# Smaller TensorE tiles in the two transform steps of an H3 long convolution, with kv kept by channels in two buffers

## The chip, the cores and the metric

The kernel runs on one core of a Trainium2 chip. The metric is the device time of one execution in microseconds; 718.91 us is the median of three executions before the change (717.91 to 720.57). Everything is computed in 32-bit floats. Where a profile is quoted, PE is TensorE's matmuls, PEld its weight loads, DVE VectorE, ACT ScalarE, POOL GpSimd, and SP the engine whose queue issues most of the DMAs.

## The reference

The input `q` has S = 2048 tokens and D = 640 channels. The kernel computes an H3 block (a causal long convolution per channel, gated) and then a mixer MLP over the token axis, both modulated by vectors worked out from `c`. The part that the change touches is the first:

```
h  = layernorm(q) * (1 + ca) + sa
kv = (short causal convolution of k with shift_k, 4 taps) * v
y  = causal convolution over all 2048 tokens of kv with ssm_k, channel by channel,  + kv * ssm_D
x  = q + ga * h * y
out = x + gb * MLP_over_tokens(layernorm(x) * (1 + cb) + sb)
```

The reference does the long convolution with a real FFT of length 4096. The MLP has 1728 hidden units with a tanh-GELU.

## The kernel before

**The order of the work.** The order of all instructions is written by hand: each engine runs its own queue in the order in which the Python code issues it, and the SP queue issues DMAs in that order too. The 640 channels are taken in NC = 5 chunks of 128. The loop of line 511 does one chunk per iteration c: it transforms chunk c and brings it back, and in between does part of the work of chunk c + 1 (step one of its transform) and of chunk c + 2 (its kv). After that loop come the layernorm, the two products of the MLP with their split weights (from line 656 on, which the change does not touch) and the output.

**The transform.** 2048 tokens are written as 64 x 32 (n1 = 64 rows on the partitions, n2 = 32), and the length-4096 transform becomes two matmul steps with constants.

- `step1(side, t)`, line 210: for kv (side 0, the tile X) and for ssm_k (side 1, a permuted copy KSP in the tile P), 32 column groups i, eight for each t. Each group has 2 x 64 rows on the partitions (two halves of the channels) and 64 columns, and is the stationary operand, [128 rows, 64 columns]; the moving operand is a 128-column half of F1, one call for the real and one for the imaginary part. So there are 4 x 8 x 2 = 64 calls per side and chunk. In X the 64 columns of a group lie 32 elements apart; KSP has them side by side. ACT evicts each t (1024 columns) into the tile Z (line 220).
- `f2(g)`, line 224, is step two: for each of eight frequencies k1, for real and imaginary part and for two channel halves h, one call with a stationary [128 rows, 64 columns] block of the constant W2 and 64 moving columns out of Z. W2 is block-diagonal over two halves c of the columns, so half of each block is zeros. One f2(g) has 32 calls; eight g make a chunk. ACT copies the ssm_k half of the result to `kt` (line 238); DVE multiplies it with the kv half in two operations of 512 columns into `p` (mul, line 242); `add` (line 248) subtracts and adds real and imaginary parts into `y`, two operations of 256 columns on POOL, except for the last g of a chunk after the first, which DVE does.
- `i2(r)`, line 255, and `i1(half)`, line 273, are the inverse steps. i2 uses tiles of 32 rows by 128 columns, i1 of 64 rows by 64 columns, with 64 moving columns in both. Row tiles at the same columns write to different PSUM banks there (the offsets 512 * (qd % 2) and 512 * e).

A call of `pe.matmul` on 32-bit floats becomes two weight loads and two matmuls in the trace: f2 makes 1280 calls in the five chunks, and the profile counts 2560 matmuls on line 234.

**kv and the other work.** `kv_ops(g)` (line 172) is eight operations of 512 columns on DVE for one of four token groups g; the last writes into X. All four groups of a chunk are 32 operations, handed out between other work by `dv(n)` (line 506); `kv_loads` (line 185) issues the k and v loads of the next chunk as the groups finish. For the first chunks POOL does group 2, with its own copy of the taps (PW). There is one X: the kv of the next chunk may only be written when step one of this one has read it. `load_ks` (line 150) loads ssm_k of a chunk into KSR (half of the tile T_aux) in pieces of 32 floats; `perm_add` adds ssm_D to the first tap (on POOL, in iteration c after g = 3), and `perm` (line 163) copies KSR to KSP on ACT. The next `load_ks` follows in each iteration (line 626) as soon as `perm` has read KSR. `gate` (line 299) multiplies the convolution with h on DVE and adds it to x on POOL. `load_rows` fetches MLP weights into T_aux near the end of the loop.

**The start.** Lines 443 to 502 load and compute kv of chunks 0 and 1, load W2 (two tiles of 2 MB), q and four fifths of the first half of `w_mod` (`mod_load`, two pieces of it into the tile that later takes the constant V1). V1 (2 MB, used by i1) is loaded in iteration 0 at line 561, after those pieces have been used.

Of the kernel before, what the change touches and what calls it, by code (L numbers as in the profile page):

```python
# [20 lines left out]
def _constants():  # L21
# [9 lines left out]
    w2 = np.zeros((2, 32, 2, 64, 2, 2, 32))  # L31
    for c in range(2):
        w2[0, :, c, :, 0, c] = np.cos(ang)
        w2[1, :, c, :, 0, c] = -np.sin(ang)
        w2[0, :, c, :, 1, c] = np.sin(ang)
        w2[1, :, c, :, 1, c] = np.cos(ang)
# [8 lines left out]
    return {"small": small.astype(np.float32), "w2": w2.reshape(128, 8192).astype(np.float32),  # L45
# [4 lines left out]
def mixer_kernel(ctx: ExitStack, tc: tile.TileContext, q, k, v, shift_k, ssm_k, ssm_D, w1, b1, w2, b2, c,  # L50
# [38 lines left out]
    KSP = P.rearrange("p (i m) -> p i m", i=32)  # L89
# [8 lines left out]
    W2 = [t.rearrange("p (k m) -> p k m", m=64) for t in T_w2]  # L98
# [64 lines left out]
    def perm(c):  # L163
        act.activation(KSP.rearrange("p i (n e) -> p i e n", e=2),
                       KSR.rearrange("p (e i n) -> p i e n", e=2, i=32), AF.Copy)

# [5 lines left out]
    def kv_ops(g, eng=dve):  # L172
# [8 lines left out]
        ops.append(lambda: TT(eng, X.rearrange("p (n i) -> p n i", i=64)[:, 8 * g:8 * g + 8], S_,  # L181
# [13 lines left out]
    def kv(c_next, gs=((0,), (1,), (2,), (3,))):  # L195

        ops = []
        for gl in gs:
            o = kv_ops(gl[0])

            def end(gl=gl, last=o.pop()):
                last()
                if c_next is not None:
                    for g in gl:
                        kv_loads(c_next, g)
            ops += o + [end]
        return ops


    def step1(side, t, later=False):  # L210

        ps = psum()
        for a in range(8):
            i = 8 * t + a
            lhs = KSP[:, i] if side else X.rearrange("p (m i) -> p i m", i=32)[:, i]
            o = 512 * (a % 2) + 128 * (a // 2)
            for ri in range(2):
                pe.matmul(ps[64 * ri:64 * ri + 64, o:o + 128], lhs, F1[:, 128 * ri:128 * ri + 128], start=True,  # L218
                          stop=True)
# [4 lines left out]
    def f2(g):  # L224

        ps = psum()
        for kk in range(8):
            k1 = 8 * g + kk
            for ri in range(2):
                for h in range(2):  # L230
                    o = 128 * kk + 64 * ri
                    rhs = bass.AP(tensor=T_z.tensor, offset=T_z.offset + 128 * h + 2 * k1,
                                  ap=[T_z.ap[0], [256, 32], [1, 2]])
                    pe.matmul(ps[64 * h:64 * h + 64, o:o + 64], W2[k1 // 32][:, 2 * (k1 % 32) + ri], rhs, start=True, stop=True)  # L234
# [13 lines left out]
        def add(eng=pool):  # L248
            for ri, t, op in ((0, pa, ALU.subtract), (1, pb, ALU.add)):
# [216 lines left out]
    run(kv_ops(2, pool))  # L466
    run(kv_ops(0))
    kv_loads(1, 0)
    run(kv_ops(1))
    kv_loads(1, 1)  # L470
    kv_loads(1, 2)
    run(kv_ops(3))
    sync.dma_start(T_w2[0], c_w2[:, 0:4096], max_dma_last_dim=4096)
    kv_loads(1, 3)
    sync.dma_start(T_w2[1], c_w2[:, 4096:8192], max_dma_last_dim=4096)
# [6 lines left out]
    perm(0)  # L482
    all_taps()
    load_taps(2)
    for t in range(4):
        step1(0, t)
    run(kv_ops(2, pool))
    run(kv_ops(0))
    run(kv_ops(1))
    for t in range(4):  # L490
        step1(1, t)
# [7 lines left out]
    pl = [three(t) for t in (T_aux, T_aux[:, 2048:3968], T_v1, T_v1[:, 1920:3840], P)]  # L499

    for kk in range(4):
        mod_load(0, kk, (T_aux[:, 0:1920], T_aux[:, 2048:3968], T_v1[:, 0:1920], T_v1[:, 1920:3840])[kk])

    fill = kv_ops(3)
# [6 lines left out]
    for c in range(NC):  # L511
# [26 lines left out]
        pa_next(dve if c else pool)  # L538
# [5 lines left out]
        if c and c + 2 < NC:  # L544
            taps()
            if c + 3 < NC:
                load_taps(c + 3)
        if c == 0:
            mod_load(0, 4, P[:, 0:1920])
            for t in range(4):  # L550
                step1(0, t)
# [9 lines left out]
            sync.dma_start(T_v1[:, 0:4096], c_v1, max_dma_last_dim=4096)  # L561
# [16 lines left out]
            run(kv_ops(2, pool))  # L578
# [5 lines left out]
            perm(1)  # L584
            load_ks(2)
            run(ac[8:16])
            run(po[0:2])
            fill.extend(kv(3, ((0,), (1, 2), (3,))))
        elif cn is not None:
            for t in range(2):  # L590
                step1(0, t)
            perm(cn)
# [492 lines left out]
```

## Time and profile before

| | us |
|---|---|
| median of three executions | 718.91 (717.91 to 720.57) |
| the profiled execution | 722.7 |
| its span, first to last instruction | 720.8 |
| loop over the chunks, from f2 of chunk 0 (42.0) to the end of f2 of chunk 4 (288.4) | 246.4 |
| of it f2, five times (25.0, 19.5, 19.0, 18.9, 19.1) | 101.5 |

The profile is of one execution. A row of a group says line, engine, operation, output<-inputs, shape, count | busy time, mean ns of one | idle time of the engine before it, and what ended that. For matmuls the shape starts with rows*columns of the stationary tile. In the timeline a row is: start, length, engine, line, operation, count, and in brackets the engine's idle time before it and what ended it; "issue" there means that the engine waited for nothing that the profile shows. In the table of stretches (windows) a row has: the stretch and its length; then busy time and count of each engine, the granted TensorE clock (1.00 is full speed), the busy share of the DMA engines and the GB/s moved.

### The profile page before, as it was taken

How to read it: one execution, taken by the hardware profiler on the slowest of the kernel's cores; microseconds unless marked ns; L12 is line 12 of the kernel's file. 1: busy time of each engine (PE TensorE's matmuls, PEld its weight loads, DVE VectorE, ACT ScalarE, POOL GpSimd, SP SyncE). 2: the span in 40 equal slices, each digit the busy share in tenths (PEclk: the TensorE clock that was granted, in tenths of full speed). 3: DMA queues.
4: the chain of work that ended last, by engine and by line, in shares of the span. 5: the costliest groups of instructions: out<-in, count | busy, mean ns of one | idle time of the engine just before them, and what ended most of it. 6: DMA issues, size and time to landing. Idle time of an engine off the chain costs nothing.

```text
span 720.8 us, 20751 instructions
## 1 busy us (share of the span) xinstructions
PE 656.0 (91%) x9131; PEld 632.6 (88%) x9131; DVE 492.6 (68%) x861; ACT 297.4 (41%) x465; POOL 154.6 (21%) x135
## 2 busy tenths in 40 slices
PE   0797968999999999998889999999999989999997
PEld 0797758989999989777889999999999989999997
DVE  7666748969879638788894313212389768888887
ACT  0432564645745545446766223112244222333221
POOL 5187038715626328100010000000000000000000
PEclk9998889999999899879999999999999999999999
DMA  9979998527233522351203543352263423455510
GB/s 185 243 223 223 304 235 172 116 52 164 57 68 87 168 55 70 112 133 44 53 7 59 101 75 60 76 100 59 59 183 102 141 96 123 130 159 175 159 45 37
DMA packets 165903, 84.89 MB, mean 118 GB/s; under 512 B 88979, under 2 KB 157366, under 8 KB 165814
## 3 DMA queue, kind: packets, MB, share of 16 engines
q1 hardware_dynamic: 161266, 82.27, 46.1%
q10 hardware_dynamic: 4548, 1.31, 1.0%
q8 instruction: 71, 1.16, 0.7%
q14 instruction: 18, 0.15, 0.1%
HBM read 73.07 MB, written 10.49 MB: 116 GB/s over the span
## 4 chain that ended last, share of the span: by engine, by line
PE 54%; DVE 23%; ACT 6%; issue 5%; POOL 5%; DMA 4%; SPq 2%; ACTq 0%; DVEq 0%; POOLq 0%
PE pst L432 21%; PE pst L218 8%; PE pst L234 8%; PE pst L1026 7%; PE pst L263 5%; DVE m_w L59 4%; POOL y L59 4%; DVE m_x L59 3%; PE pst L282 3%; DVE tap L59 2%; ACT m_w L939 2%; PE pst L951 2%; DVE kt L59 2%; DVE m_x L960 1%; DVE m_v L59 1%
## 5 line engine op out<-in xcount | busy, mean ns | idle before, releaser
L234 PE MATMUL pst<-z,w 128*64 128x64 f32 x2560 | 96.8, 241 | 11.2 <-ACT z L220 6.1
L234 PEld LDWEIGHTS pst<-z,w 128*64 128x64 f32 x2560 | 95.4, 142 | 12.9 <-ACT z L220 7.3
L59 POOL TENSOR_TENSOR y<-p 128x256 f32<-128x256 f32 x72 | 90.6, 1315 | 27.2 <-DVE p L59 26.7
L59 DVE TENSOR_TENSOR p<-pst,kt 128x512 f32<-128x512 f32 x80 | 52.7, 688 | 29.6 <-ACT kt L238 20.9
L218 PE MATMUL pst<-v,x 128*64 128x128 f32 x640 | 48.3, 315 | 23.2 <-DVE x L59 23.2
L218 PEld LDWEIGHTS pst<-v,x 128*64 128x64 f32 x640 | 46.3, 222 | 23.7 <-POOL t L457 23.2
L220 ACT ACTIVATE z<-pst 128x1024 f32<-128x1024 f32 x40 | 45.7, 1144 | 48.9 <-PE pst L218 31.1
L238 ACT ACTIVATE kt<-pst 128x512 f32<-128x512 f32 x40 | 25.1, 628 | 58.5 <-PE pst L234 39.6
L830 ACT ACTIVATE pst<-pst,sm 128x640 f32<-128x640 f32 x14 | 10.7, 767 | 85.9 <-PE pst L432 85.9
L263 PEld LDWEIGHTS pst<-v,y 32*128 32x128 f32 x1280 | 40.5, 197 | 5.9 <-POOL y L59 2.5
L263 PE MATMUL pst<-v,y 32*128 32x64 f32 x1280 | 42.6, 283 | 2.6 <-DVE y L59 1.5
L951 PE MATMUL pst<-r_z,m_w 128*128 128x320 f32 x222 | 42.8, 312 | 2.1 <-DVE m_w L59 1.6
L218 PE MATMUL pst<-v,p 128*64 128x128 f32 x640 | 37.7, 274 | 2.4 <-issue 2.2
L939 ACT ACTIVATE m_w<-m_v 128x896 fp32r<-128x896 f32 x24 | 22.2, 949 | 42.4 <-DVE m_v L59 29.4
L218 PEld LDWEIGHTS pst<-v,p 128*64 128x64 f32 x640 | 35.2, 137 | 3.6 <-issue 3.1
L951 PEld LDWEIGHTS pst<-r_z,m_w 128*128 128x128 f32 x222 | 34.8, 188 | 3.7 <-DVE m_w L59 2.9
L59 DVE TENSOR_TENSOR tap<-tap,kt 128x512 f32<-128x512 f32 x51 | 35.5, 697 | 1.3
L59 DVE TENSOR_TENSOR kt<-in,tap 128x512 f32<-128x512 f32 x51 | 35.0, 687 | 1.4
L59 DVE TENSOR_TENSOR m_w<-m_v,m_w 128x896 fp32r<-128x896 f32 x24 | 26.0, 1087 | 10.4 <-ACT m_w L939 10.4
L271 ACT ACTIVATE z<-pst 128x512 f32<-128x512 f32 x38 | 21.2, 657 | 26.3 <-PE pst L263 26.3
L282 PEld LDWEIGHTS pst<-z,v 64*64 64x64 f32 x1280 | 23.7, 154 | 8.4 <-issue 6.3
L282 PE MATMUL pst<-z,v 64*64 64x64 f32 x1280 | 25.3, 240 | 6.1 <-DMA v<-in_const_v_dram 3.0
(277 smaller groups left out, 1425.7 us busy)
## 6 DMA issues: line engine op xcount, KB each, us to landing
x<-in_B_w_dram SPq DMA_DIRECT2D x22, 512.0 KB
m_v<-in_B_w_dram SPq DMA_DIRECT2D x15, 384.0 KB
x<-in_B_w_dram SPq DMA_DIRECT2D x14, 384.0 KB
aux<-in_A_ssm_k_dram SPq DMA_DIRECT2D x10, 512.0 KB
in<-in_A_k_dram SPq DMA_DIRECT2D x36, 128.0 KB
in<-in_A_v_dram SPq DMA_DIRECT2D x36, 128.0 KB
m_x<-xs SPq DMA_DIRECT2D x28, 160.0 KB
out_dram<-m_x SPq DMA_DIRECT2D x28, 160.0 KB
```

Of the source, the lines that this page charges most:

```text
L59: TT = lambda eng, o, a, b, op: eng.tensor_tensor(o, a, b, op=op)
L218: pe.matmul(ps[64 * ri:64 * ri + 64, o:o + 128], lhs, F1[:, 128 * ri:128 * ri + 128], start=True, stop=True)
L220: evac = lambda: act.activation(Z[:, side, t].rearrange("p a k e -> p e a k"), ps.rearrange("p (e a k) -> p e a k", a=8, e=2), AF.Copy)
L234: pe.matmul(ps[64 * h:64 * h + 64, o:o + 64], W2[k1 // 32][:, 2 * (k1 % 32) + ri], rhs, start=True, stop=True)
L238: act.activation(kt.rearrange("p (m i) -> p m i", i=32), pv[:, :, 1], AF.Copy)
L263: pe.matmul(pp[qd // 2][:, o:o + 64], Y[p, ri, i:i + 2].rearrange("p i k -> p (i k)"), V2[p, 64 * ri:64 * ri + 64], start=ri == 0, stop=ri ...
L271: act.activation(o, i, AF.Copy)
L282: pe.matmul(ps[64 * b:64 * b + 64, 512 * e + 64 * jj:512 * e + 64 * jj + 64], V1[p, ri, n2], T2[p, :, 32 * ri + n2], start=ri == 0, stop=r ...
L432: pe.matmul(ps[0:m, h, 0:320], w_.bitcast(F32R), r_[:, 320 * h:320 * h + 320].bitcast(F32R), start=first and i == 0, stop=last and i == 2)
L939: act.activation(W[n][0].bitcast(F32R), a(w_), AF.Copy)
L951: pe.matmul(bank[n], w[:, i].bitcast(F32R), r.bitcast(F32R), start=i == 0 and k == 0, stop=i == 6 and k == 2)
L1026: pe.matmul(acc[s][:, h, 0:320], w[:, f_].bitcast(F32R), u[r + h].bitcast(F32R), start=f_ == 0 and k == 0, stop=f_ == NF - 1 and k == 2)
```

## The change

It changes the layout of the two transform steps and moves work around them:

- **Step two** uses stationary tiles of 64 rows by 32 columns. The zero halves of W2 are gone (the constant is 128 x 4096, 2 MB, in the first of the two W2 tiles). Each call is split in two, one for each half e, at tile positions (row 64 e, column 64 h + 32 e): 64 calls for each g in place of 32. The two halves e write the same PSUM columns on different partitions.
- **Step one** uses tiles of 128 rows by 32 columns at four column positions, so that Z comes out in the order that step two needs: 128 calls per side and chunk in place of 64. Its ssm_k side reads KSR itself; `perm` and KSP are gone.
- **kv** is written by channels (the 32 columns of a group side by side), into two buffers in turn: X, and the second half of the former second W2 tile.
- `add` is split: POOL subtracts, DVE adds, for every g. In iterations 1 and 2 POOL also does kv group 2 of the chunk after next, so DVE has 24 kv operations there and not 32.
- `load_ks` of chunk c + 2 is issued at the end of iteration c, after step one has read KSR; the last `load_rows` moves likewise. The pieces of `w_mod` go to the free W2 tile and to X, so V1 is loaded right behind them, ahead of the loop.

The diff, without its context lines:

```diff
-    w2 = np.zeros((2, 32, 2, 64, 2, 2, 32))
+    w2 = np.zeros((2, 2, 32, 64, 2, 32))
...
-        w2[0, :, c, :, 0, c] = np.cos(ang)
-        w2[1, :, c, :, 0, c] = -np.sin(ang)
-        w2[0, :, c, :, 1, c] = np.sin(ang)
-        w2[1, :, c, :, 1, c] = np.cos(ang)
+        w2[c, 0, :, :, 0] = np.cos(ang)
+        w2[c, 1, :, :, 0] = -np.sin(ang)
+        w2[c, 0, :, :, 1] = np.sin(ang)
+        w2[c, 1, :, :, 1] = np.cos(ang)
...
-    return {"small": small.astype(np.float32), "w2": w2.reshape(128, 8192).astype(np.float32),
+    return {"small": small.astype(np.float32), "w2": w2.reshape(128, 4096).astype(np.float32),
...
-    KSP = P.rearrange("p (i m) -> p i m", i=32)
...
-    W2 = [t.rearrange("p (k m) -> p k m", m=64) for t in T_w2]
+    W2 = T_w2[0].rearrange("p (k m) -> p k m", m=32)
...
+    XK = [t.rearrange("p (i n) -> p i n", n=32) for t in (X, T_w2[1][:, 2048:4096])]
...
-    def perm(c):
-        act.activation(KSP.rearrange("p i (n e) -> p i e n", e=2),
-                       KSR.rearrange("p (e i n) -> p i e n", e=2, i=32), AF.Copy)
...
-    def kv_ops(g, eng=dve):
+    def kv_ops(g, cc, eng=dve):
...
-        ops.append(lambda: TT(eng, X.rearrange("p (n i) -> p n i", i=64)[:, 8 * g:8 * g + 8], S_,
+        ops.append(lambda: TT(eng, XK[cc % 2].rearrange("p i n -> p n i")[:, 8 * g:8 * g + 8], S_,
...
-    def kv(c_next, gs=((0,), (1,), (2,), (3,))):
+    def kv(cc, c_next, gs=((0,), (1,), (2,), (3,))):
...
-            o = kv_ops(gl[0])
+            o = kv_ops(gl[0], cc)
...
-    def step1(side, t, later=False):
+    def step1(cc, side, t, later=False):
...
-            lhs = KSP[:, i] if side else X.rearrange("p (m i) -> p i m", i=32)[:, i]
...
-            for ri in range(2):
-                pe.matmul(ps[64 * ri:64 * ri + 64, o:o + 128], lhs, F1[:, 128 * ri:128 * ri + 128], start=True,
-                          stop=True)
+            for e in range(2):
+                lhs = KSR[:, 32 * (32 * e + i):32 * (32 * e + i) + 32] if side else XK[cc % 2][:, 32 * e + i]
+                for ri in range(2):
+                    r = 64 * e + 32 * ri
+                    pe.matmul(ps[r:r + 32, o:o + 128], lhs, F1[:, 128 * ri:128 * ri + 128], start=True, stop=True,
+                              tile_position=(0, r))
...
+                o = 128 * kk + 64 * ri
...
-                    o = 128 * kk + 64 * ri
-                    rhs = bass.AP(tensor=T_z.tensor, offset=T_z.offset + 128 * h + 2 * k1,
-                                  ap=[T_z.ap[0], [256, 32], [1, 2]])
-                    pe.matmul(ps[64 * h:64 * h + 64, o:o + 64], W2[k1 // 32][:, 2 * (k1 % 32) + ri], rhs, start=True, stop=True)
+                    for e in range(2):
+                        z = T_z[64 * e:64 * e + 64]
+                        rhs = bass.AP(tensor=z.tensor, offset=z.offset + 128 * h + 2 * k1,
+                                      ap=[z.ap[0], [256, 32], [1, 2]])
+                        r = 64 * h + 32 * e
+                        pe.matmul(ps[r:r + 32, o:o + 64], W2[64 * e:64 * e + 64, 2 * k1 + ri], rhs, start=True,
+                                  stop=True, tile_position=(64 * e, r))
...
-        def add(eng=pool):
-            for ri, t, op in ((0, pa, ALU.subtract), (1, pb, ALU.add)):
+        def add():
+            for ri, t, op, eng in ((0, pa, ALU.subtract, pool), (1, pb, ALU.add, dve)):
...
-    run(kv_ops(2, pool))
-    run(kv_ops(0))
+    run(kv_ops(2, 0, pool))
+    run(kv_ops(0, 0))
...
-    run(kv_ops(1))
+    run(kv_ops(1, 0))
...
-    run(kv_ops(3))
-    sync.dma_start(T_w2[0], c_w2[:, 0:4096], max_dma_last_dim=4096)
+    run(kv_ops(3, 0))
...
-    sync.dma_start(T_w2[1], c_w2[:, 4096:8192], max_dma_last_dim=4096)
+    sync.dma_start(T_w2[0], c_w2, max_dma_last_dim=4096)
...
-    perm(0)
...
-        step1(0, t)
-    run(kv_ops(2, pool))
-    run(kv_ops(0))
-    run(kv_ops(1))
+        step1(0, 0, t)
+    run(kv_ops(2, 1, pool))
+    run(kv_ops(0, 1))
+    run(kv_ops(1, 1))
...
-        step1(1, t)
+        step1(0, 1, t)
...
-    pl = [three(t) for t in (T_aux, T_aux[:, 2048:3968], T_v1, T_v1[:, 1920:3840], P)]
+    pl = [three(t) for t in (T_aux, T_aux[:, 2048:3968], T_w2[1], X, P)]
...
-        mod_load(0, kk, (T_aux[:, 0:1920], T_aux[:, 2048:3968], T_v1[:, 0:1920], T_v1[:, 1920:3840])[kk])
...
-    fill = kv_ops(3)
+        mod_load(0, kk, (T_aux[:, 0:1920], T_aux[:, 2048:3968], T_w2[1][:, 0:1920], X[:, 0:1920])[kk])
+    sync.dma_start(T_v1[:, 0:4096], c_v1, max_dma_last_dim=4096)
...
+    fill = kv_ops(3, 1)
...
-        pa_next(dve if c else pool)
+        pa_next()
...
+            pool.tensor_scalar(PW, TR.rearrange("p (i s) -> p s i", s=4), 1.0, None, op0=ALU.mult)
...
-                step1(0, t)
+                step1(1, 0, t)
...
-            sync.dma_start(T_v1[:, 0:4096], c_v1, max_dma_last_dim=4096)
...
-            run(kv_ops(2, pool))
+            run(kv_ops(2, 2, pool))
...
-            perm(1)
-            load_ks(2)
...
-            fill.extend(kv(3, ((0,), (1, 2), (3,))))
+            fill.extend(kv(2, 3, ((0,), (1, 2), (3,))))
...
-                step1(0, t)
-            perm(cn)
+                step1(cn, 0, t)
...
-                fill.extend(kv(c + 3 if c + 3 < NC else None))
+                run(kv_ops(2, c + 2, pool))
+                fill.extend(kv(c + 2, c + 3 if c + 3 < NC else None, ((0,), (1, 2), (3,))))
...
-            step1(0, 2)
+            step1(cn, 0, 2)
...
-            step1(0, 3)
+            step1(cn, 0, 3)
...
-        if c and c + 2 < NC:
-            load_ks(c + 2)
...
-            load_rows(1, T_aux[:, 0:2048])
...
-                k0 = step1(1, 0, True)
+                k0 = step1(cn, 1, 0, True)
...
-            step1(1, t)
+            step1(cn, 1, t)
+        if c + 2 < NC:
+            load_ks(c + 2)
...
+            load_rows(1, T_aux[:, 0:2048])
```

## The prediction, made before the change was run

> **What bounds the kernel now.** I read the page first, then the stretches of the chunk loop, the timeline of PE inside them, and the groups by form. The page has TensorE busy 91% of the span, and its second queue fetches instructions:
>
> ```profile
> PE 656.0 (91%) x9131; PEld 632.6 (88%) x9131; DVE 492.6 (68%) x861; ACT 297.4 (41%) x465; POOL 154.6 (21%) x135
> ```
> ```profile
> q8 instruction: 71, 1.16, 0.7%
> ```
>
> 9131 matmuls and 9131 weight loads in 71 packets are 257 instructions a packet (the row has packets, MB and share): one packet of 16 KB carries 256 instructions of TensorE, that is 128 matmuls with their loads. I call that a block.
>
> The iterations of chunks 1 to 3, f2 included (first table), and f2 alone (second: five rows for chunks 0 to 4):
>
> ```profile
> 117.00:167.90 50.90, 47.91 (x1280) 45.99 (x1280) 42.19 (x57) 27.52 (x42) 26.41 (x20) 1.00 0.52 110
> 167.90:217.70 49.80, 47.53 (x1282) 46.07 (x1282) 41.28 (x55) 27.60 (x42) 23.23 (x18) 1.00 0.44 92
> 217.70:269.30 51.60, 49.58 (x1280) 48.10 (x1280) 33.45 (x66) 26.71 (x41) 23.51 (x18) 0.93 0.35 101
> ```
> ```profile
> 42.00:67.00 25.00, 20.05 (x512) 19.60 (x512) 0.92 0.89 216
> 117.00:136.50 19.50, 19.37 (x512) 19.06 (x512) 1.00 0.72 158
> 167.90:186.90 19.00, 18.97 (x512) 18.88 (x512) 1.00 0.56 131
> 217.70:236.60 18.90, 18.90 (x512) 18.90 (x512) 1.00 0.35 110
> 269.30:288.40 19.10, 19.07 (x512) 18.93 (x512) 1.00 0.27 73
> ```
>
> PE is without work for only 2 to 3 us of each 50, so in this loop PE's time is the kernel's time. f2 of chunk 0 is the exception: 5 of its 25 us are idle. What ends that idle time is the key row of the whole profile. Timeline of PE, four places:
>
> ```profile
> 56.10 4.80 PE L234 MATMUL pst<-z,w 128*64 128x64 f32 x127 [1.01 <-issue]
> 64.84 2.19 PE L234 MATMUL pst<-z,w 128*64 128x64 f32 x36 [3.94 <-issue]
> ```
> ```profile
> 104.82 1.91 PE L282 MATMUL pst<-z,v 64*64 64x64 f32 x114 [0.67 <-issue]
> 106.65 1.09 PE L218 MATMUL pst<-v,p 128*64 128x128 f32 x14
> 109.25 1.97 PE L218 MATMUL pst<-v,p 128*64 128x128 f32 x32 [1.51 <-issue]
> ```
> ```profile
> 156.71 1.53 PE L218 MATMUL pst<-v,p 128*64 128x128 f32 x24 [0.72 <-issue]
> 158.17 1.75 PE L282 MATMUL pst<-z,v 64*64 64x64 f32 x104
> 160.72 0.58 PE L282 MATMUL pst<-z,v 64*64 64x64 f32 x24 [0.80 <-issue]
> ```
> ```profile
> 202.05 2.28 PE L218 MATMUL pst<-v,x 128*64 128x128 f32 x32
> 204.29 2.10 PE L282 MATMUL pst<-z,v 64*64 64x64 f32 x128
> 206.32 2.54 PE L218 MATMUL pst<-v,p 128*64 128x128 f32 x32
> ```
>
> Three pairs of stalls without any semaphore wait, and between the two of a pair lie 127, 114 + 14 = 128 and 24 + 104 = 128 matmuls: exactly one block. TensorE has run out of instructions. From the start of one block to the arrival of the next it takes 64.84 - 56.10 = 8.74 us, 109.25 - 104.82 = 4.43 us and 160.72 - 156.71 = 4.01 us, whatever the work in the block. So the supply is a period of its own, and it follows the load on the DMA engines (share in the column before the last):
>
> ```profile
> 204.20:211.00 6.80, 6.65 (x293) 6.01 (x290) 5.21 (x7) 1.25 (x2) 2.39 (x1) 1.00 0.02 6
> 156.70:160.80 4.10, 3.29 (x132) 2.98 (x136) 2.00 (x4) 0.00 (x0) 2.38 (x1) 1.00 0.94 158
> 104.80:109.30 4.50, 2.97 (x130) 2.66 (x129) 4.30 (x4) 0.25 (x1) 4.34 (x3) 1.00 0.75 169
> 56.10:64.90 8.80, 4.86 (x129) 4.71 (x130) 5.35 (x9) 1.26 (x2) 8.80 (x9) 0.90 1.03 226
> ```
>
> For idle DMA engines (share 0.02) I have the table of DMA queues between 204.5 and 211.6 us:
>
> ```profile
> q8 instruction: 3, 0.05, 3.0%
> ```
>
> Three packets start within 7.1 us, so two periods are 3.55 us each or less. There the supply is only just enough: the 32 matmuls from 206.32 take 2.54 us, those from 202.05 took 2.28. I take 3.55 us as the period with little DMA traffic, 4.0 to 4.4 with loads under way, 8.7 while the inputs of the start stream in. A block of i1 (64 x 64 tiles, the 128 matmuls from 204.29) runs in 2.10 us, so only short bursts from the stock can go at that pace. f2 today uses a block in 19.0 / 4 = 4.75 us, slower than the supply: it is not starved except in chunk 0.
>
> [...]
>
> **The change part by part.** More groups by form for the terms:
>
> ```profile
> L59 POOL TENSOR_TENSOR y<-p 128x256 f32<-128x256 f32 x72 | 90.6, 1315 | 27.2 <-DVE p L59 26.7
> L59 DVE TENSOR_TENSOR p<-pst,kt 128x512 f32<-128x512 f32 x80 | 52.7, 688 | 29.6 <-ACT kt L238 20.9 <-POOL y L59 8.6
> L218 PE MATMUL pst<-v,x 128*64 128x128 f32 x640 | 48.3, 315 | 23.2 <-DVE x L59 23.2
> ...
> L218 PE MATMUL pst<-v,p 128*64 128x128 f32 x640 | 37.7, 274 | 2.4 <-issue 2.2
> ...
> L282 PE MATMUL pst<-z,v 64*64 64x64 f32 x1280 | 25.3, 240 | 6.1 <-DMA v<-in_const_v_dram 3.0 <-ACT wb L408 1.5 <-issue 1.5
> ...
> L59 POOL TENSOR_TENSOR t<-in,t 128x512 f32<-128x512 f32 x12 | 16.1, 1354 | 33.0 <-DMA in<-in_A_k_dram 32.6
> ...
> L59 DVE TENSOR_TENSOR y<-p 128x256 f32<-128x256 f32 x8 | 9.3, 1205 | 0.0
> ```
>
> *Step two.* 512 matmuls a chunk become 1024 on tiles of a quarter of the area: eight blocks in place of four. No row shows 64 x 32 tiles; the nearest are i1's, also four at a time with 64 moving columns, 2.10 / 128 = 16.4 ns each. If only the array counted, f2 would take 1024 x 16.4 = 16.8 us, 2.2 less than now. But a block would then be used up in 2.1 us and comes every 3.55 or more. With one block in stock, f2 takes 2.1 + 7 periods. Chunk 1 (DMA share 0.72; the k and v loads of chunk 3 fall into it): at 4.1 it is 30.8, 11 more than 19.5. Chunk 2 (0.56): at 3.9 it is 29.4, 10 more. Chunks 3 and 4 (0.35, 0.27): at 3.55 it is 27.0, 8 more each. Together +37 us. The ends: all at 3.55, 27.0 x 4 = 108 against 76.5, +31; all at 4.43, 33.1 x 4 = 132, +56.
>
> *f2 of chunk 0.* Here the periods are longest. W2 is 2 MB smaller, some 10 us of traffic at 216 GB/s, and V1 comes earlier, but q and w_mod still stream in. With one block in stock, two periods of 8.7 and five of about 5 (between 4.43 and 8.74, as the traffic thins out) it is 2.1 + 17.5 + 25 = 45 against 25: +20. The start of it: step one of chunk 0 now needs four blocks in place of two, at periods over 4 us, +2. Against that, the wait of i1 for V1 (3.0 in the row of L282) goes, -3, and step one of chunk 1 has about 1 to gain. Sum +18; ends +4 (periods of 4.43 throughout: 33 - 25 = 8, less 4) and +36 (8.74 for four more of the periods).
>
> *Step one.* Twice the matmuls, each half as wide, so array time stays where the weights lie side by side: the ssm_k side has 37.7 / 640 = 59 ns, and the kv side's 48.3 / 640 = 75 ns falls towards that with the new layout. Worth about 16 ns x 128 = 2 us a chunk for chunks 1 to 4; chunk 1's share is in the sum above. But one side is now two blocks in 256 x 29.5 ns = 7.6 us, 3.8 a block: just at the supply. What is left of an iteration besides f2 is eight blocks (256 matmuls each of kv side, ssm_k side, i2 and i1) in 31 us, 3.9 each, with i1's bursts starved between them as at 156.71 and 160.72. I take +2 for chunk 1, +1 for chunk 2, 0 for chunk 3: +3, ends -5 and +15.
>
> *The additions, kv and their engines.* A g of f2 is one block, so 3.55 us or more. In it DVE has two products and one addition, 2 x 0.69 + 1.2 = 2.6 us, and POOL one subtraction, 1.3. Both wait for PE then, so these moves cost nothing in the forecast; what covers them is the starved f2. In chunk 1 DVE has 16 kv operations besides (11 us, sum 32): level with the 31 of f2, nothing added. POOL's kv group 2, eight times 1.35 = 11 us, stands in its queue ahead of the gates' additions to x, whose products need i1 about 20 us after f2: hidden. The strided write of kv by channels has no row of its own form on DVE; between the contiguous 0.69 and 1.2 for the strided y it costs 0 to 0.5 us for one operation in eight, under the same cover. `perm` leaves ACT, busy 27 of 50 us: nothing.
>
> *load_ks.* Issued a chunk ahead before, now at the start of f2; behind it SP holds the k and v loads, and `perm_add` on POOL after the fourth f2 waits for it, with all later subtractions. Its transfer is seen in the stretches around the load issued at 194.46:
>
> ```profile
> 194.40:202.40 8.00, 8.00 (x223) 7.75 (x218) 7.21 (x6) 3.83 (x7) 0.00 (x0) 1.00 0.84 135
> 202.40:210.20 7.80, 7.65 (x287) 7.02 (x285) 5.21 (x7) 3.05 (x5) 2.38 (x1) 1.00 0.02 6
> ```
>
> It is over in 8 us (share 0.84, then 0.02). Four g take 2.1 + 3 x 3.55 = 12.7 us, so the wait is covered; but its traffic now lies on f2's first blocks, one reason for 3.9 to 4.1 above. The extra changes of tile shape cost less than 0.1 us each by the rows at 202.05 and 204.29, which follow without a gap.
>
> **Sum.** 18 + 37 + 3 = +58 us on the profiled execution's 722.7 gives 781; that execution lies 3.8 above the median, so the forecast is 718.9 + 58 = 777.
>
> **The rivals.** [...] (2) *The supply does not bind and DVE paces f2*: chunk 1 loses 10 (32 us of DVE work against 19.5), the others regain it: 0, 719. (3) *The two row halves of f2 do not run together* because they write the same PSUM columns, which i1 and i2 avoid: at 4 x 16.4 = 66 ns a matmul, f2 takes 67 us, +48 a chunk, about 960. [...] If the four tiles ran two at a time, f2 would take 34 us, and the time would be near the forecast for another reason.
>
> **How the numbers follow.** The forecast's own range is the sum of its ends: from -5 + 31 + 4 = +30 to +107, and 10 lower for a better start: 739 to 826. Chances: forecast 0.80, rival 1 0.11, rival 2 0.05, rival 3 0.04. The range 739 to 826 holds nearly all of the first, which is the 8 in 10. A measurement of this kernel can tell about 0.5% (3.6 us) from no change: faster 0.12, same 0.05, slower 0.83.
>
> **What would show it.** Right: "issue" as what ends the idle time of f2's matmuls in most blocks, matmuls in bursts of 128 starting 3.5 to 4.5 us apart, f2 of 27 to 31 us in chunks 1 to 4 and 35 to 60 in chunk 0, and about 30 more packets on the instruction queue. Wrong: f2 under 20 us, its matmuls evenly spaced, or waits on DVE's y or p at its end.

## The result, and the profile after

The kernel after the change takes 803.1 us (median of four executions, 801.87 to 806.06); the kernel before, run beside it, 719.74 us (717.91 to 720.57). The ratio is 1.1146, with a 95% interval of 1.1104 to 1.1188: slower by 83 us. The profiled execution took 803.56 us with a span of 801.8, so 81.0 us of span against the execution profiled before. Medians here and below are of all executions; a ratio leaves out those more than 1.5% above the fastest of their kernel.

The page of the kernel after: engines and instruction queue.

```profile
PE 664.0 (83%) x12971; PEld 633.4 (79%) x12971; DVE 529.4 (66%) x877; ACT 285.4 (36%) x460; POOL 145.1 (18%) x121
...
q8 instruction: 101, 1.65, 0.8%
```

TensorE has 3840 more matmuls and as many more loads, 7680 instructions, which are 30 blocks of 256; the queue has 30 more packets (101 against 71). PE's busy time rose by only 8 us. What grew is the time in which it has nothing to do, and the group of step two says what ends it:

```profile
L236 PE MATMUL pst<-z,w 64*32 64x64 f32 x5120 | 108.2, 245 | 68.4 <-issue 60.4
...
L266 PE MATMUL pst<-v,y 32*128 32x64 f32 x1280 | 43.9, 287 | 0.5 <-ACT z L219 0.4
```

In the first row, 68.4 us of idle time stand before the matmuls of step two, and 60.4 of it ended with no semaphore at all; the second row, i2, is for later. The timeline of PE in step two of chunks 0, 1, 3 and 4 shows the form of it:

```profile
46.29 4.58 PE L236 MATMUL pst<-z,w 64*32 64x64 f32 x221 [1.16 <-ACT z L219]
57.27 3.63 PE L236 MATMUL pst<-z,w 64*32 64x64 f32 x128 [6.40 <-issue]
65.93 3.64 PE L236 MATMUL pst<-z,w 64*32 64x64 f32 x128 [5.03 <-issue]
...
148.30 2.76 PE L236 MATMUL pst<-z,w 64*32 64x64 f32 x140 [1.22 <-ACT z L219]
152.14 2.49 PE L236 MATMUL pst<-z,w 64*32 64x64 f32 x128 [1.08 <-issue]
156.15 2.46 PE L236 MATMUL pst<-z,w 64*32 64x64 f32 x128 [1.52 <-issue]
...
276.27 5.05 PE L236 MATMUL pst<-z,w 64*32 64x64 f32 x256 [1.25 <-ACT z L219]
283.05 2.55 PE L236 MATMUL pst<-z,w 64*32 64x64 f32 x128 [1.73 <-issue]
289.18 3.63 PE L236 MATMUL pst<-z,w 64*32 64x64 f32 x128 [3.58 <-issue]
294.42 6.44 PE L236 MATMUL pst<-z,w 64*32 64x64 f32 x255 [1.60 <-DVE p L59]
301.96 2.64 PE L236 MATMUL pst<-z,w 64*32 64x64 f32 x127 [1.09 <-issue]
306.06 2.64 PE L236 MATMUL pst<-z,w 64*32 64x64 f32 x128 [1.46 <-issue]
309.62 0.29 PE L236 MATMUL pst<-z,w 64*32 64x64 f32 x2 [0.92 <-issue]
...
340.88 5.12 PE L236 MATMUL pst<-z,w 64*32 64x64 f32 x250 [1.23 <-ACT z L219]
348.35 2.51 PE L236 MATMUL pst<-z,w 64*32 64x64 f32 x128 [2.35 <-issue]
...
371.58 0.34 PE L236 MATMUL pst<-z,w 64*32 64x64 f32 x8 [1.02 <-issue]
```

Each burst is one block of 128 matmuls (a record is missing here and there). In chunk 1 a burst takes 2.4 to 2.5 us and starts 3.8 to 4.2 us after the one before it. Stretches of the loop: f2 of chunk 0, the rest of its iteration, and f2 of chunks 1, 3 and 4 (length, then busy time and count of PE, PEld, DVE, ACT and POOL, granted clock, DMA share, GB/s):

```profile
46.30:92.20 45.90, 24.41 (x1024) 22.60 (x1024) 19.33 (x27) 4.22 (x7) 7.50 (x7) 0.78 0.79 228
92.20:148.30 56.10, 43.63 (x1097) 35.77 (x1097) 40.52 (x77) 25.75 (x42) 20.95 (x13) 0.82 0.42 95
148.30:178.35 30.05, 19.95 (x1028) 18.62 (x1032) 27.62 (x36) 9.52 (x21) 10.73 (x9) 1.00 0.60 122
...
276.30:309.90 33.60, 23.14 (x1028) 21.46 (x1032) 16.59 (x22) 9.63 (x21) 8.82 (x9) 0.85 0.45 122
...
340.90:371.90 31.00, 20.55 (x1025) 19.09 (x1026) 21.42 (x52) 10.06 (x25) 7.61 (x7) 1.00 0.29 72
```

PE is busy for 24.41 of the 45.9 us and about 20 of 30. With the stretches of the other iterations, cut in the same way, the 81.0 us divide so:

| stage | before | after | difference | forecast |
|---|---|---|---|---|
| up to f2 of chunk 0 | 42.0 | 46.3 | +4.3 | +2 |
| f2 of chunk 0 | 25.0 | 45.9 | +20.9 | +20 |
| rest of iteration 0 | 50.0 | 56.1 | +6.1 | -4 |
| f2 of chunk 1 | 19.5 | 30.05 | +10.6 | +11 |
| f2 of chunk 2 | 19.0 | 29.9 | +10.9 | +10 |
| f2 of chunks 3, 4 | 18.9, 19.1 | 33.6, 31.0 | +26.6 | +16 |
| rest of iterations 1 to 3 | 31.4, 30.8, 32.7 | 34.15, 33.9, 31.0 | +4.1 | +3 |
| from the end of f2 of chunk 4 | 432.4 | 429.9 | -2.5 | 0 |

### The profile page after: what moved, and what is told of

The parts are those of the page before. It is cut to its first block, busy times and chain, and to the rows that moved or that the text cites. A ratio compares the mean times of both kernels' runs of the same rounds, so it can differ in the third digit from the quotient of the medians.

```text
span 801.8 us, 28419 instructions
## 1 busy us (share of the span) xinstructions
PE 664.0 (83%) x12971; PEld 633.4 (79%) x12971; DVE 529.4 (66%) x877; ACT 285.4 (36%) x460; POOL 145.1 (18%) x121
## 3 DMA queue, kind: packets, MB, share of 16 engines
q10 hardware_dynamic: 4548, 1.31, 0.9%
q8 instruction: 101, 1.65, 0.8%
## 4 chain that ended last, share of the span: by engine, by line
PE 35%; DVE 17%; issue 6%; ACT 5%; POOL 0%; DMA 0%; DVEq 0%; ACTq 0%
PE pst L435 19%; PE pst L1026 6%; PE pst L236 4%; DVE m_w L59 4%; DVE m_x L59 2%; ACT m_w L939 2%; PE pst L266 2%; DVE m_v L59 2%; PE pst L951 2%; PE pst L217 1%; DVE m_x L960 1%; DVE m_p L59 1%; PE pst L285 1%; PE tap L345 1%; ACT z L274 1%
## 5 line engine op out<-in xcount | busy, mean ns | idle before, releaser
L236 PE MATMUL pst<-z,w 64*32 64x64 f32 x5120 | 108.2, 245 | 68.4 <-issue 60.4
L236 PEld LDWEIGHTS pst<-z,w 64*32 64x32 f32 x5120 | 100.3, 118 | 76.8 <-issue 67.4
L59 POOL TENSOR_TENSOR y<-p 128x256 f32<-128x256 f32 x40 | 47.6, 1190 | 154.5 <-DVE p L59 152.8
L217 PE MATMUL pst<-v,aux 128*32 128x128 f32 x1280 | 42.1, 287 | 12.2 <-issue 8.4
L217 PEld LDWEIGHTS pst<-v,aux 128*32 128x32 f32 x1280 | 38.1, 116 | 14.6 <-issue 10.7
L59 DVE TENSOR_TENSOR y<-p 128x256 f32<-128x256 f32 x40 | 47.4, 1194 | 0.0
L217 PE MATMUL pst<-v,x 128*32 128x128 f32 x768 | 25.2, 289 | 26.2 <-DVE x L59 24.6
L217 PEld LDWEIGHTS pst<-v,x 128*32 128x32 f32 x768 | 22.9, 117 | 27.1 <-issue 26.5
L939 ACT ACTIVATE m_w<-m_v 128x896 fp32r<-128x896 f32 x24 | 22.2, 949 | 42.4 <-DVE m_v L59 29.4
L59 POOL TENSOR_TENSOR t<-in,t 128x512 f32<-128x512 f32 x20 | 30.1, 1513 | 21.0 <-DMA in<-in_A_k_dram 20.1
L59 DVE TENSOR_TENSOR tap<-tap,kt 128x512 f32<-128x512 f32 x45 | 31.4, 698 | 1.3
L59 DVE TENSOR_TENSOR kt<-in,tap 128x512 f32<-128x512 f32 x45 | 30.8, 685 | 1.3
```

Source lines behind the costliest of these rows:

```text
L59: TT = lambda eng, o, a, b, op: eng.tensor_tensor(o, a, b, op=op)
L217: pe.matmul(ps[r:r + 32, o:o + 128], lhs, F1[:, 128 * ri:128 * ri + 128], start=True, stop=True, tile_position=(0, r))
L236: pe.matmul(ps[r:r + 32, o:o + 64], W2[64 * e:64 * e + 64, 2 * k1 + ri], rhs, start=True, stop=True, tile_position=(64 * e, r))
L939: act.activation(W[n][0].bitcast(F32R), a(w_), AF.Copy)
```

## The experiments

The theory: the supply of instruction blocks to TensorE sets the pace of step two. The rivals: PSUM banks shared by row halves, DVE's pace, and costs of the other parts (kv by channels, no `perm`, the divided additions). Each ratio is against the kernel before, run on the same chip.

**More instructions in the kernel before (nops4).**

```diff
+                    for _ in range(4):
+                        pe.nop(nofuse=True)
```

> The kernel before with four empty instructions (no-operations) on TensorE's queue behind each call of f2, nothing else changed: f2 has the instruction count of the changed kernel (eight blocks of 256 per chunk) with the old 128 x 64 tiles, banks, layout and engines. Theory (the instruction supply sets the time): f2 of chunks 1 to 4 goes from 19 to 28-32 us each and that of chunk 0 from 25 to about 45, with idle time that nothing but 'issue' ends once per block; the kernel takes 775 to 800. Rival (the small tiles, their shared banks or the moved work cost the time): empty instructions cost next to nothing, 719 to 725.

Measured 722.26 us, ratio 1.0014 (0.9983 to 1.0046). Nothing follows: the profile counts 9131 matmuls and 20751 instructions, exactly as before, so it shows none of the empty instructions, and f2 of chunks 1 to 3 took 19.58, 19.01 and 19.00 us without a stall on "issue". It is a repeat of the kernel before. A run that adds instructions and no work for the array is therefore missing; the next two change the number of instructions together with the matmuls or the weight loads.

**Twice the instructions (twice_instr).** The kernel after, with each matmul of step two issued twice.

```diff
-                        pe.matmul(ps[r:r + 32, o:o + 64], W2[64 * e:64 * e + 64, 2 * k1 + ri], rhs, start=True,
-                                  stop=True, tile_position=(64 * e, r))
+                        for _ in range(2):
+                            pe.matmul(ps[r:r + 32, o:o + 64], W2[64 * e:64 * e + 64, 2 * k1 + ri], rhs, start=True,
+                                      stop=True, tile_position=(64 * e, r))
```

> The changed kernel with every call of f2 issued twice: sixteen blocks a chunk, same result. Theory (supply): each added block costs a full period of 3.5 to 4.2 us though its matmuls run in 2.5: +28 to +34 us a chunk, 945 to 980 in all. Rival (the time is that of the bursts on the array, and the idle time between them belongs to the steps, not to the blocks): each added block costs 2.5 us, +20 a chunk, about 903.

Measured 946.31 us (943.25 to 949.37), ratio 1.3137 (1.3029 to 1.3246). That is 143 us for 40 more blocks (141 instruction packets against 101), 3.6 us each; a burst of 128 takes 2.5 us here, so the time of the array alone would have been 100. The run also has what the kernel before couldn't show, a long stretch in which step two runs and no load does. The stretch, and the table of DMA queues inside it:

```profile
82.90:121.40 38.50, 25.39 (x1278) 23.71 (x1277) 14.86 (x20) 3.10 (x5) 5.29 (x5) 1.00 0.02 4
```
```profile
q8 instruction: 10, 0.16, 1.9%
q1 hardware_dynamic: 1, 0.00, 0.0%
```

Ten instruction packets and one of 0.00 MB in 38.5 us: a block every 3.85 us on DMA engines that do nothing else. The single gaps in it run from 3.45 to 4.29 us, and in chunk 4 of the same run, at a DMA share of 0.09, 14 gaps make 51.8 us, 3.70 each.

**Half the instructions (half_instr).** Each call takes the moving columns of two frequencies at once (128 columns) with the weights of the first, so the odd frequencies' own weights are left out.

```diff
-        for kk in range(8):
+        for kk in range(0, 8, 2):
...
-                                       ap=[z.ap[0], [256, 32], [1, 2]])
+                                       ap=[z.ap[0], [256, 32], [1, 4]])
-                        pe.matmul(ps[r:r + 32, o:o + 64], W2[64 * e:64 * e + 64, 2 * k1 + ri], rhs, start=True,
+                        pe.matmul(ps[r:r + 32, o:o + 128], W2[64 * e:64 * e + 64, 2 * k1 + ri], rhs, start=True,
```

> The changed kernel with half as many calls in f2, each with 128 moving columns in place of 64: same tiles, positions, banks and columns streamed through the array, half the instructions (four blocks a chunk). It leaves out the odd frequencies' own weights (the even ones' stand in for them), so its output differs. Theory (supply): the supply alone would allow 2.5 + 3 x 3.9 = 14 us a chunk; then DVE's products and additions (2.5 us a step) pace f2 at 20 to 22 us, against 30 to 34; chunk 0 falls from 46 to about 25; 735 to 755 in all. Rival (tiles, banks or array time): f2 stays near 30 us, 790 or more.

Measured 757.93 us (752.55 and 763.32), ratio 1.0522 (1.0397 to 1.0647), 3 us over the upper end: 45 us of the 83 go with 20 of the blocks (81 packets against 101), though as many columns are multiplied. f2 itself takes 29.9, 22.6, 15.2, 19.7 and 18.9 us in the five chunks of the profiled execution, 106.3 together, against 170.4 in the kernel after and 101.5 before: of the 69 us that f2 had grown by, 64 go with the blocks. Some 24 come back elsewhere (this execution, 763.32 us, lies only 40 under that of the kernel after): the rest of iterations 1 and 2 takes 39.7 and 39.3 us in place of 34.15 and 33.9, with waits for DVE and POOL (in iteration 1 of 1.69 us for p and of 0.80 and 0.98 for y) that the kernel after hasn't, and what follows f2 of chunk 4 takes 442.1 in place of 429.9, which no run explains. In chunk 1, where f2 still took 22.6 us, its timeline shows what is late next, and the stretches of f2 in chunks 1 and 2 show how busy DVE is (third engine):

```profile
141.12 1.72 PE L236 MATMUL pst<-z,w 64*32 64x128 f32 x53 [0.48 <-issue]
144.48 1.95 PE L236 MATMUL pst<-z,w 64*32 64x128 f32 x64 [1.63 <-DVE p L59]
148.79 3.12 PE L236 MATMUL pst<-z,w 64*32 64x128 f32 x64 [2.36 <-DVE p L59]
```
```profile
131.90:154.50 22.60, 16.74 (x512) 15.03 (x512) 22.19 (x32) 9.53 (x21) 6.05 (x7) 0.92 0.75 150
194.20:209.40 15.20, 14.54 (x514) 14.07 (x516) 13.78 (x20) 9.54 (x21) 7.56 (x8) 1.00 0.83 157
```

After five of the eight g the stalls on "issue" end and DVE's p ends the wait instead, with DVE busy 22.2 of the 22.6 us of that f2. In chunk 2 DVE has less to do (13.78 us), and f2 takes 15.2, near the 14 that the supply alone was given. The second rival's mechanism is real, but it stands behind the supply.

**Other banks (banks).** The kernel after, with the calls reordered: the half e = 1 works four frequencies away from e = 0, so the row halves that run together write to different PSUM banks (columns 512 apart).

```diff
-        for kk in range(8):
-            k1 = 8 * g + kk
+        for kb in range(8):
...
+                        kk = (kb + 4 * e) % 8
+                        k1, o = 8 * g + kk, 128 * kk + 64 * ri
```

> The changed kernel with the calls of f2 in another order: the row half e = 1 works four frequencies away from e = 0, so the two row halves that run together write different PSUM banks; same calls, same results. Theory (supply): 803 within 4 us, f2 30 us a chunk; if the shared bank lengthens the bursts, they fall from 2.5 us per 128 matmuls towards i1's 2.1, and the idle time after them grows by as much. Rival (shared banks hold the row halves up): f2 falls well below 25 us a chunk and the kernel to 775 or less.

Measured 805.2 us (799.09 to 805.7), ratio 1.1142 (1.1082 to 1.1202): no difference. The group of step two in this run:

```profile
L236 PE MATMUL pst<-z,w 64*32 64x64 f32 x5120 | 110.4, 248 | 69.4 <-issue 59.0 <-ACT z L219 6.1 <-DVE y L59 3.8
```

248 ns a matmul against 245: here the shared bank costs nothing on different partitions. The third rival has no part in this case.

**Later V1 (v1_late).** The kernel after, with V1 loaded behind the last piece of `w_mod`.

```diff
-    sync.dma_start(T_v1[:, 0:4096], c_v1, max_dma_last_dim=4096)
...
             mod_load(0, 4, P[:, 0:1920])
+            sync.dma_start(T_v1[:, 0:4096], c_v1, max_dma_last_dim=4096)
```

> The changed kernel with one edit: V1 (2 MB) is loaded behind the last piece of w_mod in iteration 0, so its traffic falls behind f2 of chunk 0 and not into it. If the period of the instruction supply follows the load on the DMA engines, the blocks of f2 that start between 66 and 84 us, now 7.3, 6.4 and 4.2 us apart, come 4 to 5 us apart: f2 of chunk 0 takes 40 to 42 us in place of 45.9, and the kernel 797 to 801. If the traffic has no part in it (the rival), f2 of chunk 0 stays within 1 us of 45.9 and the kernel at 802 to 805. A wait of i1 for V1 of more than 1 us would mean that the load was moved too far.

Measured 798.65 us (796.45 to 808.0), ratio 1.1122 (1.0994 to 1.1249), which can't be told from the 803.1. The expectation missed where it counts: f2 of chunk 0 took 46 us again. Its length hides what moved, though, since it began 1.65 us earlier (44.64 against 46.29). Three bursts came at the same times in both kernels, within 0.3 us (57.01, 65.67 and 72.92 against 57.27, 65.93 and 73.19); the next came 1.8 us earlier (77.76 against 79.59), and the last 1.5. Blocks of f2, as stretches from one arrival to the next; the kernel after:

```profile
57.30:65.90 8.60, 3.60 (x128) 3.40 (x128) 2.94 (x4) 0.60 (x1) 1.11 (x1) 0.50 1.03 225
...
73.20:79.60 6.40, 3.57 (x128) 3.33 (x130) 2.93 (x4) 0.60 (x1) 1.10 (x1) 0.73 1.03 402
79.60:83.80 4.20, 3.36 (x128) 3.12 (x127) 2.41 (x4) 0.60 (x1) 1.06 (x1) 0.59 0.51 200
83.80:87.60 3.80, 2.46 (x131) 2.30 (x133) 2.56 (x4) 0.60 (x1) 1.05 (x1) 1.00 0.02 4
...
152.10:156.20 4.10, 2.54 (x132) 2.36 (x135) 3.79 (x7) 1.52 (x4) 1.81 (x2) 1.00 0.90 142
```

And with V1 later:

```profile
72.90:77.80 4.90, 3.68 (x131) 3.43 (x134) 2.82 (x4) 0.60 (x1) 1.12 (x1) 0.50 0.57 217
77.80:81.60 3.80, 3.51 (x132) 3.32 (x134) 1.91 (x4) 0.60 (x1) 1.00 (x1) 0.59 0.01 4
81.60:85.80 4.20, 2.42 (x127) 2.23 (x128) 3.83 (x6) 0.61 (x1) 1.12 (x2) 1.00 0.02 4
```

The column before the last is the DMA share. Where V1's traffic is gone, one block comes 4.9 us after the last and not 6.4, and after that there is nothing to gain: 3.8 us at a share of 0.01 and 4.2 at 0.02, 4.1 at 0.90. That one gap is all that this run shows of the traffic's part. The period doesn't follow the load step by step, as the prediction had it. In these rows it is 3.8 to 4.2 us at shares up to 0.90 (142 GB/s), 4.9 at 0.57 (217 GB/s), and 6.4 to 8.6 where the engines are full (1.03, 225 to 402 GB/s). A gap of 6.2 us at a share of 0.89, with 317 GB/s (chunk 3, shown below), says that the share alone doesn't tell.

**kv by channels alone (kv_channels).** The kernel before, with X laid out so that the 64 columns of a group lie side by side, and W2's rows in that order.

```diff
-        ops.append(lambda: TT(eng, X.rearrange("p (n i) -> p n i", i=64)[:, 8 * g:8 * g + 8], S_,
-                              VX[:, 8 * g:8 * g + 8], ALU.mult))
+        ops.append(lambda: TT(eng, X.rearrange("p (i e n) -> p n e i", e=2, i=32)[:, 8 * g:8 * g + 8], four(S_),
+                              four(VX[:, 8 * g:8 * g + 8]), ALU.mult))
...
-            lhs = KSP[:, i] if side else X.rearrange("p (m i) -> p i m", i=32)[:, i]
+            lhs = KSP[:, i] if side else X[:, 64 * i:64 * i + 64]
```

> The kernel before with one part of the change: kv is written by channels, so that the 64 stationary columns of a group of step one lie side by side; tiles of 128 x 64 and the rest stay. Expected from the row of the kv side (75 ns a matmul against 59): 2 us less per chunk for four or five chunks, 709 to 713. Rival (DVE's strided write, or the wait for DVE and POOL at i2, takes it back): 717 to 721.

Measured 730.14 us (727.21 to 738.17), ratio 1.0108 (1.0044 to 1.0171): slower by 1%, though step one has what it was promised. Its row in the kernel before has 48.3 us; in this run the groups by form have

```profile
L219 PE MATMUL pst<-v,x 128*64 128x128 f32 x640 | 43.0, 296 | 25.5 <-DVE x L59 24.9 <-DVE p L59 0.5
...
L59 DVE TENSOR_TENSOR x<-tap,in 128x512 f32<-128x512 f32 x17 | 19.8, 1164 | 12.1 <-PE pst L219 11.7
```

and the second row's counterpart before is

```profile
L59 DVE TENSOR_TENSOR x<-tap,in 128x512 f32<-128x512 f32 x17 | 11.7, 690 | 9.7 <-PE pst L218 9.4
```

PE gains 5 us and DVE pays 8 for the strided write (1164 ns against 690). Then PE is early and has to wait for y; the timeline of PE behind f2 of chunk 2, and the stretch of i2 in it:

```profile
190.62 1.97 PE L219 MATMUL pst<-v,x 128*64 128x128 f32 x32 [0.23 <-DVE p L59]
194.56 7.14 PE L264 MATMUL pst<-v,y 32*128 32x64 f32 x128 [1.98 <-DVE y L59]
```

```profile
194.60:201.60 7.00, 6.94 (x128) 6.74 (x128) 6.79 (x9) 1.91 (x1) 0.00 (x0) 0.54 0.50 80
```

After 1.98 us without work the 128 matmuls of i2 took 7.14 us, with a granted clock of 0.54 (the second fence); the next 128 took 3.86. Over the whole run, i2 has 6.0 us more busy time and 3.4 us more idle time before it than in the kernel before (48.6 and 6.0 against 42.6 and 2.6). The faster step came back as a wait and a slow clock.

**And no permutation (no_perm).** The same, with ssm_k loaded in the order of use, `perm` gone and the load behind step one.

```diff
-    def perm(c):
-        act.activation(KSP.rearrange("p i (e n) -> p i e n", e=2),
-                       KSR.rearrange("p (e i n) -> p i e n", e=2, i=32), AF.Copy)
...
+        if c + 2 < NC:
+            load_ks(c + 2)
```

> As kv_channels, and without the permutation of ssm_k: it is loaded in the order that step one reads, step one reads it where it lies, and the load of the next chunk comes at the end of the iteration, as in the change; 128 x 64 tiles and one kv buffer stay. Theory: taking the copy off ACT gains nothing, and the late load is close to the additions of the fourth f2 step (8 us of transfer against 9.5 us): 0 to +4 against kv_channels. Rival (the late load stalls POOL and with it f2): +6 or more.

Measured 736.12 us (728.09 to 737.4), ratio 1.0174 (1.0094 to 1.0254): no gain either. The interval overlaps that of kv_channels, so whether the late load adds 0 to 4 us or 6, expectation or rival, stays open. Step two of chunk 1 now waits for DVE, as PE's timeline of this run has it:

```profile
131.06 2.55 PE L230 MATMUL pst<-z,w 128*64 128x64 f32 x64 [0.66 <-DVE p L59]
135.70 2.55 PE L230 MATMUL pst<-z,w 128*64 128x64 f32 x64 [2.08 <-DVE p L59]
```

**The additions alone (split_adds).** The kernel before; POOL subtracts and DVE adds for g = 3, 5 and 7.

```diff
-            for ri, t, op in ((0, pa, ALU.subtract), (1, pb, ALU.add)):
+            for ri, t, op, eng in ((0, pa, ALU.subtract, pool), (1, pb, ALU.add, dve if g in (3, 5, 7) else pool)):
```

> The kernel before with one part of the change in small: in three of eight f2 steps (the fourth, sixth and last) DVE does the addition and POOL only the subtraction; for the last step that replaces two additions on DVE by one on each. Expected: POOL's chain through f2 shortens by about 4 us a chunk, so that i2 no longer waits for y (0.7 to 0.8 us in chunks 2 and 3): 714 to 718. Rival (DVE becomes late, above all in chunk 1 with its 16 kv operations): 719 to 725.

Measured 720.87 us, ratio 0.9998 (0.9969 to 1.0027): no difference. i2 still waits 0.43 and 0.89 us in chunks 2 and 3, now for POOL's y, and step one of chunk 1 waits 1.31 us for DVE's p.

**Both, in three divisions (kv_split, kv_split2, kv_split3).** kv by channels with DVE taking the additions of g = 3, 5, 7; then of 2, 4, 6 with the last g on DVE alone; then that from chunk 2 on only.

```diff
+            for ri, t, op, eng in ((0, pa, ALU.subtract, e), (1, pb, ALU.add, dve if c > 1 and g in (2, 4, 6) else e)):
```

> kv_channels and split_adds together, on the kernel before. In kv_channels TensorE's step one got 2 us a chunk faster, i2 then waited 1 to 2 us for DVE's and POOL's additions, and the granted clock fell to half after these waits, for 10 us. Theory: with the additions ready earlier the wait and the fall of the clock go and the 2 us a chunk remain: 706 to 712. Rival (the additions are still late): 719 or more.

> The kernel before, with kv by channels and with the additions divided anew: the last g of a chunk on DVE alone as before (on POOL in chunk 0), and of the others DVE takes the addition of g = 2, 4 and 6. POOL's queue then ends with one subtraction of 1.3 us for g = 6 and not with those of g = 6 and 7. If the time that step one saves went into i2's wait for POOL's y, that wait (1.4 to 1.6 us) goes and the kernel takes 712 to 718. If the gain is lost to something else (DVE's own queue, or a slower clock after any wait), 719 to 725.

> The kernel before with kv by channels and the additions divided as in the run before it, but DVE takes the additions of g = 2, 4 and 6 only from chunk 2 on. In the run before it, step two of chunk 1 lost 2.5 us to waits for DVE's p and y, which is busy there with 32 kv operations as well. If that is all that took the gain of step one, the kernel takes 716 to 719, 0.3 to 0.6% under the kernel before. If in chunk 1 the wait moves back to POOL's y (1.5 us or more), 719 to 722 and no difference.

Measured 723.02, 721.32 and 722.05 us, ratios 1.0058 (1.0018 to 1.0098), 0.9989 (0.9954 to 1.0024) and 1.0001 (0.9968 to 1.0035). All three missed their gain, and the first is 0.6% slower. The waits do move as planned, from POOL's y (1.58 us ahead of i2 in chunk 2 of the first) to DVE's (0.28 us there in the second), but chunk 1 then waits for DVE's p, in the third as well (0.56 us), where the divided additions had been taken off it. Whether a division exists that keeps the 5 us stays open. None of these kernels beats the one before. The first expectation has the clock fall after i2's waits in kv_channels; of its waits for y in chunks 1 to 3, one shows it: after 1.98 us in chunk 2, i2 and the 32 matmuls behind it took 10.8 us (7.14 and 3.68); after 0.58 us in chunk 1, and after 0.97 and 0.96 in chunk 3, 120 matmuls took 3.58 us each time.

## Why the prediction held, and where it didn't

*What bounds the change.* Right. Idle time that ends with "issue", bursts of 128 matmuls, 30 more packets, and the time following the number of instructions both ways (+143 us for 40 blocks more, -45 for 20 fewer, with f2 itself 64 shorter). The one block in stock was an estimate: f2 ran 221, 140, 256 and 250 matmuls before its first stall in chunks 0, 1, 3 and 4, 1.1 to 2 blocks. How much the stock can hold, no run here shows, since it need not have been full at those starts.

*The period.* This is the step that failed in size: "I take 3.55 us as the period with little DMA traffic". Three packets in 7.1 us gave one sample of two periods; the long run of step two on idle DMA engines has 3.85 for ten, with single gaps from 3.45 to 4.29, so the sample lay inside the scatter. Chunks 1 and 2 came out (30.05 and 29.9 for 30.8 and 29.4) since 3.9 and 4.1 are near what most gaps outside the heaviest loads have. Chunks 3 and 4 were costed at 3.55, 2.1 + 7 x 3.55 = 27.0, and took 33.6 and 31.0; the first lies outside the 27 to 31 us that the prediction gave as the sign of being right. In chunk 4 (rows from 340.88 on) the third block began after 7.47 us, where 7.1 was forecast; from there six periods took 371.58 - 348.35 = 23.2, 3.87 each: five of them make 1.6 more than at 3.55. And f2 isn't lined up with the blocks: its last 8 matmuls came with one more block, after 3.87 + 0.34 in place of a burst of 2.1, another 2.1. So 0.4 + 1.6 + 2.1 for the 4.0. In chunk 3 one block came after 6.1 us, 2.6 too late, with `w_mod` pieces on the DMA engines (share in the column before the last, then GB/s):

```profile
283.00:289.20 6.20, 2.57 (x131) 2.38 (x130) 3.83 (x5) 1.36 (x3) 3.12 (x4) 0.93 0.89 317
```

The next stretch, 5.2 us up to 294.42, ended with a wait for DVE's p (1.7 over a period; the burst before that product had run at a clock of 0.50 and ended at 292.8, and DVE began the product at 293.6), and the last 2 matmuls cost 1.8, much as in chunk 4; the other periods make up the rest of the 6.6.

*f2 of chunk 0.* Forecast 45, measured 45.9; the first stall ended after 11.0 us, and from there the arrivals came 8.7, 7.3, 6.4, 4.2 and twice 3.7 us apart. That is close in sum to two of 8.7 and five of 5, but not term by term, so the nearness of the sum is in part luck. The upper end of this term, +36, doesn't come out of its own numbers: six periods of 8.74 and one of 5 give +33, and the range would end at 823, not 826. The 803 lies within both.

*The rest of iteration 0.* -4 forecast, +6.1 measured. The wait for V1 (3.03) did go, as said, and one of 0.73 for ACT stands in its place. But step one got its own stalls, and a wait came for which the prediction had no term. Timeline of PE in the kernel after:

```profile
96.25 3.70 PE L217 MATMUL pst<-v,w 128*32 128x128 f32 x128 [0.79 <-issue]
102.54 1.29 PE L217 MATMUL pst<-v,w 128*32 128x128 f32 x38 [2.59 <-issue]
...
135.47 3.47 PE L217 MATMUL pst<-v,aux 128*32 128x128 f32 x116 [1.47 <-issue]
141.91 5.17 PE L217 MATMUL pst<-v,aux 128*32 128x128 f32 x128 [2.97 <-DVE aux L59]
```

Stalls of 4.85 us where there were 2.18 before, and 2.97 us until DVE's product of the gate had read a PSUM tile. That product was late since both pairs of operations ahead of the gate's two products were slow, 4.50 and 4.56 us; before, they took 2.48 and 3.45, 3.1 us less. DVE in the kernel after, and then before:

```profile
130.22 4.50 DVE L59 TENSOR_TENSOR aux<-aux,g 128x1024 f32<-128x1024 f32 x2
...
135.97 4.56 DVE L59 TENSOR_TENSOR aux<-aux,g 128x1024 f32<-128x1024 f32 x2
140.63 1.23 DVE L59 TENSOR_TENSOR aux<-pst,aux 128x1024 f32<-128x1024 f32 x1
```
```profile
99.78 2.48 DVE L59 TENSOR_TENSOR aux<-aux,g 128x1024 f32<-128x1024 f32 x2
...
105.08 3.45 DVE L59 TENSOR_TENSOR aux<-aux,g 128x1024 f32<-128x1024 f32 x2
```

POOL was at kv group 2 from 126.2 on in the kernel after, beside both pairs; before, it began at 102.5, just behind the first pair. DVE's operations of these pairs, with two inputs in SBUF, were longer beside POOL: 1.24 us for each of the first pair before, without it, 1.7 for the second, beside it, and 2.25 to 2.28 in the kernel after, beside it in both pairs. The product behind them, which reads PSUM, took 1.23 us beside POOL each time, in both kernels. Besides, 124 matmuls of i2 took 7.09 us at a clock of 0.50, for 4.85 at 0.77 before. Together: -2.3 for V1, +2.7 of stalls, +3.0 and +2.2 make 5.6 of the 6.1.

The step that failed is the -4 itself, with "step one of chunk 1 has about 1 to gain": it had no term for the stalls of chunk 1's own added blocks, nor for DVE beside POOL in the gate. POOL's group 2 stands in iteration 0 of both kernels, so this is a change of when it runs, not one of the moved pieces of work. That POOL's work and not another delay made DVE late, and so the 2.97 us, was argued from these rows, not tried.

*Step one, kv and the other engines.* The rest of iterations 1 to 3 has +4.1 for +3, but in parts +2.75, +3.1 and -1.7 for +2, +1 and 0, so the sum is nearer than its terms. The strided write of kv costs 0.35 to 0.40 us an operation in the kernel after (1037 and 1091 ns against 690; 0.47 in kv_channels), inside the 0 to 0.5 given. The starved f2 did cover it, and i2 no longer waits for y (0.5 us of idle time in its group): the same write without that cover, in kv_channels, made the kernel slower by 1%, and with less of it, in half_instr, the waits came back too. Behind `load_ks`, POOL waited once for ssm_D, 1.7 us in all, and no matmul for the load.

*The end.* The last 430 us are 2.5 shorter, which was not forecast; no run explains it.

In sum: +13.3 us over the forecast in chunk 0, +11 in f2 of the others, +1 in the rest, -2.5 at the end make the 23 us from 781 to 803.56 on the profiled execution. The mechanism, the sign and the range (739 to 826) held.

## What to carry to other kernels

Count instructions before you shrink tiles: a matmul and its load each took a place in a block of 256 here (7680 more instructions, 30 more packets), and a block came every 3.7 to 4.2 us where no heavy load ran, so step two, whose 128 matmuls ran in 2.4 to 2.6 us, was paced by the supply, whatever the array saved. Look for "issue" at equal distances in the timeline, and take the period from the longest stretch you have, not from one gap. A step that gets faster in the middle of a balanced loop must take the next engine with it, or the gain becomes a wait.

## What the hardware showed that was not expected

- The supply of instructions had a period of 3.85 us a block with nothing else on the DMA engines (3.70 in another stretch of that run), 4.1 us in a stretch with a share of 0.90 and 142 GB/s, and 6.2 to 8.6 us where large loads moved 225 to 402 GB/s.
- 128 matmuls on 64 x 32 tiles take 2.4 to 2.5 us in a burst, those on i1's 64 x 64 tiles 2.10: half the area did not make them faster. Whether the block was still coming in meanwhile, no run here shows.
- After a wait of 2 us the granted clock was 0.54 for a stretch of 7 us (kv_channels); after one of 1.58 us, in kv_split, the same 128 matmuls took 3.80 us, so not every wait is followed by it. In the starved step two a slow clock cost next to nothing in most blocks: at 0.50 a burst took 3.6 us, still less than the 3.85 until the next block.
